# P1 and P2 of the second product in two levels from the third group on, with their factors made inside the kernel

## The chip, the cores and the metric

The kernel runs on one core of a Trainium2 chip. The metric is the device time of one execution in microseconds (us). Engines are named as in the profile: PE multiplies matrices, PEld is its weight load, DVE (VectorE) does elementwise work, ACT (ScalarE) activations and copies, POOL (GpSimd) and SP (SyncE) issue DMAs here.

## The reference

Linear attention with decay over blocks of the sequence, and then a feed-forward layer with a tanh shrink (float32, B=4, H=8, S=768, D=64; 3072 tokens, model width 512, hidden width 2048):

```python
# attention, block by block, with a running state kv
intra = ((qb @ kb.T) * Dmask) @ vb
out_b = intra + (qb * lam_pow) @ kv
kv    = lam_block * kv + (kb * rev_pow).T @ vb
# x: (batch * sequence, heads * D)
h   = x @ w_in          # 3072x512 @ 512x2048: the first product
g   = h - tanh(h)
out = g @ w_out         # 3072x2048 @ 2048x512: the second product
```

## The kernel before

The tokens are taken in six groups, g = 0 to 5, of 512 tokens (128 positions of the sequence in each of the four batches). For each group the attention makes the columns of x, and then come the first and the second product. While group g is multiplied, the attention of group g+1 is worked in between its steps. Group 0 has a path of its own.

**Seven products for eight.** Each product is split in 2 x 2 blocks and done by Strassen's scheme in Winograd's form: seven products P1 to P7 of block sums instead of eight block products. The sums are S1 to S4 on one side and T1 to T4 on the other. The weights' sums for the second product are made during group 0 and lie in DRAM (`factors`).

**Two levels.** For some of the seven products the scheme is applied once more. `TWICE = (3, 5, 6, 4, 7)` names those of the second product; their finer weight factors, seven each in the order `SUB`, lie in DRAM (`fine`). P1 and P2 of the second product are done in one level.

**First product**, `up(g, u, n)`: for each of four units u (512 hidden columns) the products n. A step is four matmuls of 256 columns into one of the PSUM banks: ya or yb for the y sums by the parity of u, z for P5 and P3. DVE and ACT then finish the hidden values `hidden(g, c)` for c in 11, 12, 21, 22: L471 and L467 (for 11), L476, L477 and two L467 (for 22 and 21 after P7), L494, L467, L497 and L498 (for 12 and the sum S1 after P3). L494 reads bank z, and only then may the next unit's P5 write it. From g=2 on, P2 and P4 of the first product are done in two levels (`inner_steps`, L542) ahead of the units.

**Second product.** `down(g, n)` is the form in one level: four pieces of weights, four matmuls of 256 columns for each (L633). `down_twice(g, n, zw)` is the form in two levels: seven steps (x = 1, 2, 6, 5, 7, 3, 4 in this order), each with one piece and four matmuls of 128 columns (L686). `sums_twice` makes the token-side sums s1, s2 and a third one in place ahead of it (L670 to L672), the fourth, s4, is made in between (L691, step x = 3 waits for it), ACT copies each partial sum of y out (L689), and DVE adds the other bank to it (L696, L697).

**Pieces.** Each piece of weights is a 256 KB DMA from DRAM, issued on POOL into a ring of `RING = 7` buffers (tag `wb`), in the fixed order `stream`. A piece can be issued when the buffer that it takes is free; POOL takes its instructions in order.

**Attention of the next group.** `p0` and `p1` are its two halves: `att_transpose` (L331: DVE transposes the 32x32 blocks that SP loads as `q_blk` and `k_blk`, L342 scales), `att_scores` (L352 on PE, L356 on DVE), `att_out` (L400, L406 and copies on ACT), `att_state` (L361, L374, L379, L380). In a group g of 1 to 4, the transposes of p0 stand after unit 2 and its scores after unit 3; the rest follows P2 and later products.

**Order.** In the program P1 of the second product stands in unit 3, between P7 and P3 of the first product (it needs only `hidden(g, 11)`), then P2, P4, P5, P6, P7, P3. The program's order is an input to a scheduler, which fixes the order of instructions on each engine when the kernel is built; each engine then runs its instructions strictly in that order, and waits for the others by semaphores.

```python
INNER = (2, 4)
GI = 2
for g in range(1, NG):
    for u in range(NU):
        for n in ...:                     # up(g, u, n); at n == 1 the next unit's P1
            ...                           # u == 3: every(down(g, 1))
        if not last and u > 1:
            run(p0[u - 2:u - 1])
    every(down(g, 2))
    run(p0[2:])
    every(down_twice(g, 4, "z")); every(down_twice(g, 5, "w")); ...
```

Of the kernel before, what the change touches and what calls it, by code (L numbers as in the profile page):

```python
# [24 lines left out]
def kernel(  # L25
# [157 lines left out]

    SUB = (1, 2, 6, 5, 7, 3, 4)
    GI = 2
    TWICE = (3, 5, 6, 4, 7)
    fine = dram.tile([len(TWICE), len(SUB), 128, NU, 128], F32, name="fine")

    fine_in = dram.tile([2, 3, 128, NU, 128], F32, name="fine_in")
# [62 lines left out]
    def sums_out(kt):  # L252
        x, y = pair[kt]
        b11, b12, b21, b22, t1, t2, t4, t3 = (t[:, i] for t, n in ((x, 2), (y, 6)) for i in range(n))
        for dst, a, b in ((t1, b12, b11), (t2, b22, t1), (t3, b22, b12), (t4, b21, t2)):
            tied(kt > 1, nc.vector.tensor_tensor(dst, a, b, op=AL.subtract))
        f = factors[:].rearrange("x p k c -> p x k c")
        tied(kt > 1, nc.gpsimd.dma_start(out=f[:, 0:1, kt, :], in_=x[:, 0:1, :]))
        tied(kt > 1, nc.gpsimd.dma_start(out=f[:, 1:NX, kt, :], in_=y[:, 0:2, :]))

        for n, j in ((1, 0),) if kt % 2 == 0 else ((2, 0), (3, 1)):
            tied(kt > 1, nc.gpsimd.dma_start(out=fine[:, SUB.index(n), :, kt // 2, :].rearrange("n p c -> p n c"),
                                             in_=y[:, 1:6, ts(j, 128)]))

    def sums_fine(u):
# [234 lines left out]


    INNER = (2, 4)
    toks = {}

    def a_quarter(n, u, i, k):
# [2 lines left out]
    def inner_weights(u):  # L508
        for n in INNER:
            a11, a12, a21, a22 = (a_quarter(n, u, i, k) for i in range(2) for k in range(2))  # L510
            t = late["pool"].tile([128, 4, 128], F32, name="ws2", tag="sums", bufs=4)
            s1, s2, s4 = (t[:, x] for x in range(3))
            for dst, x, y, op in ((s1, a21, a22, AL.add), (s2, s1, a11, AL.subtract), (a21, a11, a21, AL.subtract),
                                  (s4, a12, s2, AL.subtract)):
                tc.keep_in_program_order(nc.vector.tensor_tensor(dst, x, y, op=op))
            nc.gpsimd.dma_start(out=fine_in[INNER.index(n)].rearrange("x p u c -> p u x c")[:, u], in_=t[:, 0:3])

    def inner_tokens(g):
        for n in INNER:
            x = xt[g][FACT[n][1]]  # L520
            b11, b12, b21, b22 = (x[:, k, ts(j, 128)] for k in range(2) for j in range(2))
            t = late["pool"].tile([128, 4, 128], F32, name="tt2", tag="sums", bufs=4)
            t1, t2, t4 = (t[:, x] for x in range(3))
            for dst, x, y in ((t1, b12, b11), (t2, b22, t1), (b12, b22, b12), (t4, b21, t2)):
                nc.vector.tensor_tensor(dst, x, y, op=AL.subtract)
            toks[g, n] = {1: b11, 2: b21, 3: b22, 4: t4, 5: t1, 6: t2, 7: b12}
# [32 lines left out]
    RING = 7  # L559

    def twice(g, n):
        return n in TWICE and not (g == NG - 1 and n == 3)

    def in_turn(g):

# [5 lines left out]
    def pieces_of(g):  # L571
        if g >= GI:
            yield from ((g, ("in", 4), x) for x in (6, 5, 3))
        for n in (1, 2, 4, 5, 6, 7):
            yield from ((g, n, x) for x in (SUB if twice(g, n) else range(NU)))
        if g == NG - 1:
            yield from ((g, 3, x) for x in range(NU))
            return
        for kind, x in in_turn(g):
            if kind == "down":  # L580
                yield g, 3, x
            elif x in (3, 5, 6):
                yield g + 1, ("in", 2), x

    stream = [x for g in range(1, NG) for x in pieces_of(g)]
    sent = {"n": 0}

    def piece(g, n, x):

        i = stream.index((g, n, x))  # L590
        while sent["n"] < min(i + RING, len(stream)):
            g_, n_, x_ = stream[sent["n"]]
            t = late["pool"].tile([128, 2, 256], F32, name="wb", tag="wb", bufs=RING)
            if isinstance(n_, tuple):
# [71 lines left out]

    def sums_twice(g, n):
        a11, a12, a21, a22 = quarter(g, n)
        s1, s2 = (late["pool"].tile([128, NU, 128], F32, name=f"s{x}", tag="sums", bufs=4) for x in (1, 2))
        nc.vector.tensor_tensor(s1, a21, a22, op=AL.add)  # L670
        nc.vector.tensor_tensor(s2, s1, a11, op=AL.subtract)
        nc.vector.tensor_tensor(a21, a11, a21, op=AL.subtract)  # L672
        low[g, n] = (s1, s2)

    def down_twice(g, n, zw):
        a11, a12, a21, a22 = quarter(g, n)
        s1, s2 = low.pop((g, n))
        y = bank("y2", "ya" if n in (4, 6, 3) else "yb", 1)[:, 0:128]
        zw = bank("zw", zw, 1)
        o = res[g, n] = otile(f"q{n}")  # L680
        for x, a, dst, keep in ((1, a11, y, o[:, 0:128]), (2, a12, zw[:, 0:128], None), (6, s2, y, o[:, 128:256]),
                                (5, s1, zw[:, 256:384], None), (7, a21, y, o[:, 384:512]), (3, a12, zw[:, 128:256], None),
                                (4, a22, y, o[:, 256:384])):
            wb = piece(g, n, x).rearrange("p m c -> p (m c)")
            for u in range(NU):
                nc.tensor.matmul(out=dst, lhsT=a[:, u, :], rhs=wb[:, ts(u, 128)], start=x in (1, 2) and u == 0,  # L686
                                 stop=u == NU - 1, skip_group_check=True)
            if keep is not None:
                nc.scalar.activation(keep, dst, AF.Copy)  # L689
            if x == 2:  # L690
                nc.vector.tensor_tensor(a12, a12, s2, op=AL.subtract)  # L691
            if x != STEPS[-1]:
                yield

        o5 = o.rearrange("q (i c) -> q i c", i=2)[:, :, 128:256]
        nc.vector.tensor_tensor(o5, o5, zw[:, 256:384][:, None, :].to_broadcast([128, 2, 128]), op=AL.add)  # L696
        nc.vector.tensor_tensor(o[:, 0:256], o[:, 0:256], zw[:, 0:256], op=AL.add)  # L697
        if n == 6:

            nc.vector.tensor_tensor(o, o, res[g, 1], op=AL.add)  # L700
            for x in (4, 5):
                nc.vector.tensor_tensor(res[g, x], res[g, x], o, op=AL.add)
        elif n == 7:
# [13 lines left out]
    def down_end(g):  # L717
# [4 lines left out]
        for tag, m, c0, c1 in (("z", 0, 0, 256), ("w", 1, 0, 128), ("ya", 1, 128, 256)):  # L722
# [157 lines left out]
    for g in range(1, NG):  # L880
        last = g == NG - 1
        p0, p1 = attention(g + 1) if not last else ([], [])
        for u in range(NU):
            for n in (2, 6, 5, 7, 1, 4, 3) if g < GI else (1, 7, 3) if u == 0 else (6, 5, 1, 7, 3) if u + 1 < NU else (
# [3 lines left out]
                elif u + 1 < NU:  # L888
                    up(g, u + 1, 1)
                else:  # L890
                    every(down(g, 1))
                if g == 1 and u < 2 and n == 5:
                    sums_in(u + 2)
            if g == GI - 1:
                inner_weights(u)
            if not last and u > 1:
                run(p0[u - 2:u - 1])
        if twice(g, 4):
            sums_twice(g, 4)
        every(down(g, 2))  # L900
        run(p0[2:])
        sums_twice(g, 5)
        every(down_twice(g, 4, "z") if twice(g, 4) else down(g, 4))
        run(p1[0:1])
        sums_once(g, 21, 21, 11)
        sums_twice(g, 6)
        every(down_twice(g, 5, "w"))
        run(p1[1:2])
        if twice(g, 7):
            sums_twice(g, 7)  # L910
        every(down_twice(g, 6, "z"))
        if twice(g, 3):
            sums_twice(g, 3)
        run(p1[2:])
        every(down_twice(g, 7, "w") if twice(g, 7) else down(g, 7))
        if last:
            down_end(g)
            continue
        inner_tokens(g + 1)
        p3 = down_twice(g, 3, "z") if twice(g, 3) else down(g, 3)  # L920
# [42 lines left out]
```

## Time and profile before

| | |
|---|---|
| Time, median of 3 runs | 667.03 us (665.2 to 667.34) |
| Profiled execution | 667.09 us, span 665.3 us |
| PE, DVE, ACT, POOL busy | 653.6, 480.0, 215.0, 196.0 us |
| Granted TensorE clock | 1.0 throughout |
| DMA moved | 121.74 MB, mean 183 GB/s |

The span runs from the first to the last instruction of the profiled execution; the time of an execution is 1.8 us longer. A row of the groups gives the line, the engine, the operation, what is written from what, the count, the busy time and the mean of one; two matmul records stand for one float32 matmul. In timelines the first column is the start, the second the length, and brackets give the idle time before and what ended it. Matmul records overlap, so the time of a step is read from start to start.

### The profile page before, as it was taken

The page shows a single profiled execution, that of the slowest core. Times are in us where ns is not written, and L with a number is a line of the kernel's source. Part 1 is how long each engine was busy: PE and PEld are TensorE (multiplying, and loading weights), DVE is VectorE, ACT ScalarE, POOL GpSimd, SP SyncE. Part 2 cuts the span into 40 slices and gives each one's busy share as a digit, 9 for nine tenths or more (in the row PEclk, how much of TensorE's full clock was granted, in tenths as well). Part 3 has the DMA queues.
Part 4 walks back from the last instruction along what each step waited for, and adds up shares of the span by engine and source line. Part 5 has one row for each costly group of instructions (what it writes and reads, how often), then busy time and mean ns, then how long its engine had stood idle before and what let it go on. Part 6 is the DMA issues. An engine that isn't in the chain of part 4 may idle for free.

```text
span 665.3 us, 13244 instructions
## 1 busy us (share of the span) xinstructions
PE 653.6 (98%) x4992; PEld 594.6 (89%) x4992; DVE 480.0 (72%) x869; ACT 215.0 (32%) x413; POOL 196.0 (29%) x340
## 2 busy tenths in 40 slices
PE   7899999999999999999999999999999999999998
PEld 6688888888888899888999988999988899988897
DVE  4467888997787994579895379887368877357753
ACT  4787933423321112341112342112243112233110
POOL 0001425783112445001435101254300245400261
PEclk9999999999999999999999999999999999999999
DMA  9999946997346979435899643698830676610495
GB/s 209 221 209 255 282 159 198 349 332 221 81 87 150 268 214 292 81 71 115 219 265 273 149 76 72 164 297 247 218 68 16 160 237 216 222 38 1 114 303 169
DMA packets 161006, 121.74 MB, mean 183 GB/s; under 512 B 133872, under 2 KB 135024, under 8 KB 160944
## 3 DMA queue, kind: packets, MB, share of 16 engines
q0 software_dynamic: 26400, 86.27, 41.0%
q1 hardware_dynamic: 134400, 34.64, 26.0%
q8 instruction: 39, 0.64, 0.4%
q14 instruction: 23, 0.19, 0.1%
q10 hardware_dynamic: 144, 0.00, 0.0%
HBM read 100.67 MB, written 20.19 MB: 182 GB/s over the span
## 4 chain that ended last, share of the span: by engine, by line
PE 74%; issue 9%; DVE 6%; DMA 4%; POOL 3%; SPq 2%; ACT 2%; POOLq 0%; DVEq 0%; ACTq 0%
PE y L458 13%; PE y L686 12%; PE zw L686 9%; PE z L458 8%; PE h L741 7%; PE y L542 4%; PE w L633 4%; PE y L633 4%; PE sp L352 3%; PE op L406 2%; PE z L542 2%; PE op L400 1%; PE w L542 1%; PE end L725 1%; DMA fine<-wt 1%
## 5 line engine op out<-in xcount | busy, mean ns | idle before, releaser
L598 POOL DMA_DIRECT2D wb<-fine x168 | 90.5, 538 | 137.3 <-PE y L686 60.8
L466 ACT ACTIVATE th<-g 128x512 f32<-128x512 f32 x76 | 47.6, 630 | 99.5 <-DVE g L471 34.2
L689 ACT ACTIVATE q<-y 128x128 f32<-128x128 f32 x96 | 26.6, 278 | 149.3 <-PE y L686 148.5
L458 PE MATMUL y<-xt,w 128*128 128x256 f32 x320 | 73.5, 380 | 0.0
L601 POOL DMA_DIRECT2D wb<-factors x44 | 23.8, 542 | 165.0 <-PE y L633 127.8
L458 PEld LDWEIGHTS y<-xt,w 128*128 128x128 f32 x320 | 59.9, 190 | 8.5 <-ACT g L546 0.9
L467 DVE TENSOR_TENSOR g<-g,th 128x512 f32<-128x512 f32 x76 | 52.1, 689 | 21.1 <-ACT th L466 21.0
L686 PE MATMUL y<-wb,g 128*128 128x128 f32 x456 | 60.6, 278 | 0.0
L741 PE MATMUL h<-xt,w 128*128 128x256 f32 x256 | 58.0, 383 | 2.5 <-DVE w L296 2.5
L741 PEld LDWEIGHTS h<-xt,w 128*128 128x128 f32 x256 | 47.7, 190 | 10.3 <-DVE w L296 2.9
L686 PEld LDWEIGHTS y<-wb,g 128*128 128x128 f32 x456 | 55.1, 192 | 1.3 <-issue 0.3
L686 PE MATMUL zw<-wb,g 128*128 128x128 f32 x304 | 40.3, 275 | 0.1
L458 PE MATMUL z<-tt,ws 128*128 128x256 f32 x160 | 38.1, 381 | 0.0
L458 PE MATMUL y<-tt,ws 128*128 128x256 f32 x160 | 37.8, 379 | 0.0
L458 PE MATMUL z<-xt,ws 128*128 128x256 f32 x160 | 37.8, 379 | 0.0
L686 PEld LDWEIGHTS zw<-wb,g 128*128 128x128 f32 x304 | 37.0, 192 | 0.2 <-DVE g L691 0.2
L633 PE MATMUL w<-wb,g 128*128 128x256 f32 x160 | 35.8, 382 | 0.0
L633 PE MATMUL y<-wb,g 128*128 128x256 f32 x160 | 35.3, 379 | 0.0
L356 DVE TENSOR_TENSOR ss<-sp,mask 128x512 f32<-128x512 f32 x48 | 31.1, 685 | 5.8 <-PE sp L352 5.8
L458 PEld LDWEIGHTS z<-xt,ws 128*128 128x128 f32 x160 | 30.4, 190 | 4.1
L633 PEld LDWEIGHTS y<-wb,g 128*128 128x128 f32 x160 | 30.4, 190 | 4.1
L633 PEld LDWEIGHTS w<-wb,g 128*128 128x128 f32 x160 | 30.1, 190 | 4.4
(178 smaller groups left out, 1292.8 us busy)
## 6 DMA issues: line engine op xcount, KB each, us to landing
wb<-fine POOLq DMA_DIRECT2D x168, 256.0 KB, 4.0
wb<-factors POOLq DMA_DIRECT2D x44, 256.0 KB, 4.3
v_nat<-in_v_dram SPq DMA_DIRECT2D x24, 256.0 KB, 5.2
wb<-fine_in POOLq DMA_DIRECT2D x24, 256.0 KB, 4.2
k_nat<-in_k_dram SPq DMA_DIRECT2D x20, 256.0 KB, 5.0
raw<-in_moe_w_out_dram POOLq DMA_DIRECT2D x10, 512.0 KB, 5.4
raw<-in_moe_w_in_dram SPq DMA_DIRECT2D x8, 512.0 KB, 6.1
raw<-in_moe_w_in_dram SPq DMA_DIRECT2D x16, 256.0 KB, 6.1
```

Of the source, the lines that this page charges most:

```text
L352: tied(g == 0, nc.tensor.matmul(out=sp[j][:, p, :], lhsT=kt[ts(j, 64), p, :], rhs=qt[ts(j, 64), p, :], start=True, stop=True))
L356: tied(g == 0, nc.vector.tensor_tensor(ss[:, j], sp[j], mask[:, j], op=AL.mult))
L458: nc.tensor.matmul(out=t[:, m, :], lhsT=wt[:, kt, ts(m, 128)], rhs=x[:, kt, :], start=first and m == 0 and kt == 0, stop=kt == 1, skip_gro ...
L466: nc.scalar.activation(th, src, AF.Tanh)
L467: nc.vector.tensor_tensor(dst(c), src, th, op=AL.subtract)
L542: nc.tensor.matmul(out=dst[:, ts(u, 128)], lhsT=a, rhs=b, start=x in (1, 2, 5) and u == 0, stop=True, skip_group_check=True)
L598: nc.gpsimd.dma_start(out=t.rearrange("p m c -> p (m c)"), in_=fine[TWICE.index(n_), SUB.index(x_)].rearrange("p u c -> p (u c)"))
L601: nc.gpsimd.dma_start(out=t, in_=factors[XAT[FACT[n_][1]]][:, 2 * x_:2 * x_ + 2, :])
L633: nc.tensor.matmul(out=t[:, m, :], lhsT=a[:, u, kt, ts(m, 128)], rhs=wb[:, kt, :], start=first and u == 0 and m == 0 and kt == 0, stop=u = ...
L686: nc.tensor.matmul(out=dst, lhsT=a[:, u, :], rhs=wb[:, ts(u, 128)], start=x in (1, 2) and u == 0, stop=u == NU - 1, skip_group_check=True)
L689: nc.scalar.activation(keep, dst, AF.Copy)
L741: tied(u == 0, nc.tensor.matmul(out=hm[c][:, m, :], lhsT=w1[u][:, i, a, ts(m, 128)], rhs=xt[0, t][:, i, :], start=m == 0 and i == 0, stop= ...
```

## The change

`TWICE` also holds 1 and 2, from g=2 on. Their factors for the second level are made in g=2 itself: the four quarters of `factors` for P1 are loaded through the ring as pieces of their own, three of them are written to `fine` as they are, four DVE subtractions make the others, and these are written too. That happens in units 1 (for P1) and 2 (for P2) of the first product, one subtraction at each of four steps. P1 and P2 then read seven pieces each. Their sums s3 and s4 get buffers of their own instead of being made in place, since their operands are needed again. The next group's first transposes stand after unit 0 and its first scores after unit 1. The banks z and w change places for the later products.

```diff
-    TWICE = (3, 5, 6, 4, 7)
+    TWICE = (3, 5, 6, 4, 7, 1, 2)
...
     def twice(g, n):
-        return n in TWICE and not (g == NG - 1 and n == 3)
+        return g >= GI if n in (1, 2) else g < NG - 1 or n != 3
...
+        if g == GI:
+            yield from ((g, ("quarter", n), x) for n in (1, 2) for x in range(4))
...
+    def factors_twice(g, n):
+
+        at, quarters = fine[TWICE.index(n)], []
+        for x, direct in enumerate((1, None, 2, 3)):
+            quarters.append(piece(g, ("quarter", n), x).rearrange("p m (v c) -> p (m v) c", v=2))
+            if direct:
+                nc.gpsimd.dma_start(out=at[SUB.index(direct)], in_=quarters[x])
+        b11, b12, b21, b22 = quarters
+        t1, t2, t4 = (late["pool"].tile([128, NU, 128], F32, name=f"wt{x}", tag="sums", bufs=SUMS) for x in (1, 2, 4))
+        for x, dst, a, b in ((5, t1, b12, b11), (6, t2, b22, t1), (7, b12, b22, b12), (4, t4, b21, t2)):
+            tc.keep_in_program_order(nc.vector.tensor_tensor(dst, a, b, op=AL.subtract))
+            nc.gpsimd.dma_start(out=at[SUB.index(x)], in_=dst)
+            yield
...
     def sums_twice(g, n):
         a11, a12, a21, a22 = quarter(g, n)
-        s1, s2 = (late["pool"].tile([128, NU, 128], F32, name=f"s{x}", tag="sums", bufs=4) for x in (1, 2))
+        s1, s2, s3 = (late["pool"].tile([128, NU, 128], F32, name=f"s{x}", tag="sums", bufs=SUMS) if x < 3 or n < 3 else a21
+                      for x in (1, 2, 3))
...
     def down_twice(g, n, zw):
...
+        s4 = late["pool"].tile([128, NU, 128], F32, name="s4", tag="sums", bufs=SUMS) if n < 3 else a12
-        y = bank("y2", "ya" if n in (4, 6, 3) else "yb", 1)[:, 0:128]
+        y = bank("y2", "ya" if n in (1, 4, 6, 3) else "yb", 1)[:, 0:128]
...
-        if n == 6:
+        if n == 2:
+            nc.vector.tensor_tensor(o, o, res[g, 1], op=AL.add)
+            store(g, 11, o)
+            sums_once(g, 11, "S1", 11)
+        elif n == 6:
...
-                    every(down(g, 1))
+                    every(down_twice(g, 1, "w") if twice(g, 1) else down(g, 1))
...
+                if g == GI and u in (1, 2) and n in (6, 5, 1, 7):
+                    if n == 6:
+                        making = factors_twice(g, u)
+                    next(making)
+                if u + 1 == NU and n == 5 and twice(g, 1):
+                    sums_twice(g, 1)
...
-            if not last and u > 1:
-                run(p0[u - 2:u - 1])
-        if twice(g, 4):
-            sums_twice(g, 4)
-        every(down(g, 2))
+            early_ = u if g >= GI else u - 2
+            if not last and 0 <= early_ < 2:
+                run(p0[early_:early_ + 1])
+        even = ("w", "z") if twice(g, 2) else ("z", "w")
+        if twice(g, 2):
+            sums_twice(g, 2)
+        sums_twice(g, 4)
+        every(down_twice(g, 2, "z") if twice(g, 2) else down(g, 2))
...
-        every(down_twice(g, 4, "z") if twice(g, 4) else down(g, 4))
+        every(down_twice(g, 4, even[0]))
```

More of the change, by code (lines that the diff above doesn't have):

```diff
@@ L261, in sums_out @@
         for n, j in ((1, 0),) if kt % 2 == 0 else ((2, 0), (3, 1)):
-            tied(kt > 1, nc.gpsimd.dma_start(out=fine[:, SUB.index(n), :, kt // 2, :].rearrange("n p c -> p n c"),
+            tied(kt > 1, nc.gpsimd.dma_start(out=fine[0:5, SUB.index(n), :, kt // 2, :].rearrange("n p c -> p n c"),
                                              in_=y[:, 1:6, ts(j, 128)]))
@@ L502 @@
     INNER = (2, 4)
+    SUMS = 4
     toks = {}
@@ L510, in inner_weights @@
             a11, a12, a21, a22 = (a_quarter(n, u, i, k) for i in range(2) for k in range(2))
-            t = late["pool"].tile([128, 4, 128], F32, name="ws2", tag="sums", bufs=4)
+            t = late["pool"].tile([128, 4, 128], F32, name="ws2", tag="sums", bufs=SUMS)
             s1, s2, s4 = (t[:, x] for x in range(3))
@@ L521, in inner_tokens @@
             b11, b12, b21, b22 = (x[:, k, ts(j, 128)] for k in range(2) for j in range(2))
-            t = late["pool"].tile([128, 4, 128], F32, name="tt2", tag="sums", bufs=4)
+            t = late["pool"].tile([128, 4, 128], F32, name="tt2", tag="sums", bufs=SUMS)
             t1, t2, t4 = (t[:, x] for x in range(3))
@@ L593, in piece @@
             t = late["pool"].tile([128, 2, 256], F32, name="wb", tag="wb", bufs=RING)
-            if isinstance(n_, tuple):
+            if isinstance(n_, tuple) and n_[0] == "quarter":
+                i, j = divmod(x_, 2)
+                nc.gpsimd.dma_start(out=t.rearrange("p m (v c) -> p (m v) c", v=2), in_=factors[
+                    XAT[FACT[n_[1]][1]]].rearrange("p (u m) c -> p u m c", m=2)[:, :, i, ts(j, 128)])
+            elif isinstance(n_, tuple):
                 nc.gpsimd.dma_start(out=t.rearrange("p m c -> p (m c)"), in_=fine_in[
@@ L668, in sums_twice @@
         a11, a12, a21, a22 = quarter(g, n)
-        s1, s2 = (late["pool"].tile([128, NU, 128], F32, name=f"s{x}", tag="sums", bufs=4) for x in (1, 2))
+        s1, s2, s3 = (late["pool"].tile([128, NU, 128], F32, name=f"s{x}", tag="sums", bufs=SUMS) if x < 3 or n < 3 else a21
+                      for x in (1, 2, 3))
         nc.vector.tensor_tensor(s1, a21, a22, op=AL.add)
         nc.vector.tensor_tensor(s2, s1, a11, op=AL.subtract)
-        nc.vector.tensor_tensor(a21, a11, a21, op=AL.subtract)
-        low[g, n] = (s1, s2)
+        nc.vector.tensor_tensor(s3, a11, a21, op=AL.subtract)
+        low[g, n] = (s1, s2, s3)
     def down_twice(g, n, zw):
         a11, a12, a21, a22 = quarter(g, n)
-        s1, s2 = low.pop((g, n))
-        y = bank("y2", "ya" if n in (4, 6, 3) else "yb", 1)[:, 0:128]
+        s1, s2, s3 = low.pop((g, n))
+        s4 = late["pool"].tile([128, NU, 128], F32, name="s4", tag="sums", bufs=SUMS) if n < 3 else a12
+        y = bank("y2", "ya" if n in (1, 4, 6, 3) else "yb", 1)[:, 0:128]
         zw = bank("zw", zw, 1)
-        o = res[g, n] = otile(f"q{n}")
+        o = res[g, n] = late["pool"].tile([128, 512], F32, name="o11", tag="o11", bufs=1) if n == 2 else otile(f"q{n}")
         for x, a, dst, keep in ((1, a11, y, o[:, 0:128]), (2, a12, zw[:, 0:128], None), (6, s2, y, o[:, 128:256]),
-                                (5, s1, zw[:, 256:384], None), (7, a21, y, o[:, 384:512]), (3, a12, zw[:, 128:256], None),
+                                (5, s1, zw[:, 256:384], None), (7, s3, y, o[:, 384:512]), (3, s4, zw[:, 128:256], None),
                                 (4, a22, y, o[:, 256:384])):
@@ L690, in down_twice @@
             if x == 2:
-                nc.vector.tensor_tensor(a12, a12, s2, op=AL.subtract)
+                nc.vector.tensor_tensor(s4, a12, s2, op=AL.subtract)
             if x != STEPS[-1]:
@@ L721, in down_end @@
         wbs = [piece(g, 3, u) for u in range(NU)]
-        for tag, m, c0, c1 in (("z", 0, 0, 256), ("w", 1, 0, 128), ("ya", 1, 128, 256)):
+        for tag, m, c0, c1 in (("w", 0, 0, 256), ("z", 1, 0, 128), ("ya", 1, 128, 256)):
             t = bank("end", tag, 1)[:, 0:c1 - c0]
@@ L906 @@
         sums_twice(g, 6)
-        every(down_twice(g, 5, "w"))
+        every(down_twice(g, 5, even[1]))
         run(p1[1:2])
-        if twice(g, 7):
-            sums_twice(g, 7)
-        every(down_twice(g, 6, "z"))
+        sums_twice(g, 7)
+        every(down_twice(g, 6, even[0]))
         if twice(g, 3):
@@ L914 @@
         run(p1[2:])
-        every(down_twice(g, 7, "w") if twice(g, 7) else down(g, 7))
+        every(down_twice(g, 7, even[1]))
         if last:
@@ L919 @@
         inner_tokens(g + 1)
-        p3 = down_twice(g, 3, "z") if twice(g, 3) else down(g, 3)
+        p3 = down_twice(g, 3, even[0])
         p2 = inner_steps(g + 1, 2, "yb")
```

## The prediction

> **What bounds the kernel now.** I read the page's busy times and costliest groups, then PE's timeline through one group, then DVE's busy time by stage, DVE's timeline, and the DMA issues.
>
> ```profile
> PE 653.6 (98%) x4992; PEld 594.6 (89%) x4992; DVE 480.0 (72%) x869; ACT 215.0 (32%) x413; POOL 196.0 (29%) x340
> ```
>
> PE is busy for 653.6 of 665.3 us, so the time is PE's work plus its pauses. PE's timeline (start, us, engine, line, operands, count; two records per matmul) in the third group, g=2:
>
> ```profile
> 299.64 1.89 PE L458 MATMUL y<-xt,w 128*128 128x256 f32 x8
> 301.37 7.07 PE L633 MATMUL y<-wb,g 128*128 128x256 f32 x32
> 308.27 1.89 PE L458 MATMUL z<-xt,ws 128*128 128x256 f32 x8
> 310.09 2.06 PE L352 MATMUL sp<-qt,kt 64*128 64x128 f32 x32
> 312.08 7.17 PE L633 MATMUL w<-wb,g 128*128 128x256 f32 x32
> 319.18 1.10 PE L400 MATMUL op<-qd,state 64*64 64x128 f32 x32
> ...
> 323.04 1.16 PE L686 MATMUL y<-wb,g 128*128 128x128 f32 x8
> 324.04 1.06 PE L686 MATMUL zw<-wb,g 128*128 128x128 f32 x8
> 324.93 1.06 PE L686 MATMUL y<-wb,s 128*128 128x128 f32 x8
> ```
>
> P1 runs 301.37 to 308.27: 16 matmuls of 256 columns, 0.432 us each. A step of the two-level form is four matmuls of 128 columns in 0.893 us (324.04 to 324.93). PE has no gap of note. DVE by stage (stage, its length, busy, clock, DMA share, GB/s):
>
> ```profile
> 274.00:301.00 27.00, 19.92 (x31) 1.00 0.32 59
> 301.00:323.00 22.00, 20.64 (x35) 1.00 0.58 132
> ```
>
> Where P1 and P2 run, DVE is busy 20.64 of 22 us: it has 1.4 us to give. Its timeline there gives the prices:
>
> ```profile
> 304.11 0.68 DVE L476 TENSOR_TENSOR g<-g,y 128x512 f32<-128x512 f32 x1
> 304.70 0.68 DVE L477 TENSOR_TENSOR g<-g,y 128x512 f32<-128x512 f32 x1
> ...
> 310.20 0.69 DVE L494 TENSOR_TENSOR g<-g,z 128x512 f32<-128x512 f32 x1 [0.60 <-PE z L458]
> 311.64 0.69 DVE L467 TENSOR_TENSOR g<-g,th 128x512 f32<-128x512 f32 x1 [0.76 <-ACT th L466]
> ```
>
> One operation starts every 0.60 us; 0.72 if it reads the one before (L497 to L498, 290.56 to 291.28); add, tanh, subtract takes 1.44 from start to start (310.20 to 311.64).
>
> **What is removed: PE.** P1 or P2 costs 16 x 0.432 = 6.90 us now and 7 x 0.893 = 6.25 in two levels. That is 0.65 per product, 1.30 per group, 5.2 over groups 2 to 5. The weight loads of the new form (28 x 0.192 = 5.4 us by the L686 rows) stay under it.
>
> In the Trainium skill, "TensorE: Matmul & The Clock Gate", section "Back-to-back issue gap", speaks against this: in a stream of load and matmul pairs it gives about 81 ns per matmul at 128 columns and 131 at 512. Interpolated (an estimate from that page), 128 columns would cost 0.83 of 256, and a two-level product 28 x 0.83 x 0.432 = 10.0 us, 25 us lost in all.
>
> The trace decides otherwise: 0.223 us against 0.432, a ratio of 0.52, in rows of this same code (L686).
>
> **What is added: DVE.** Per group eight operations of 128x512 (s1, s2, s3, s4 of P1 and of P2) at 0.60, and four PSUM additions of 256 columns at about 0.4 (L696, L697): 6.4 us. Moved out to units 0 and 1 are six transposes and scalings (300.53 to 304.11, 3.6 us) and four mask products (2.4 us). The stage would hold 20.64 + 6.4 - 6.0 = 21.0 us of DVE work in 22 - 1.3 = 20.7. DVE is as long as PE there, so every place where PE needs a DVE result must be walked, in the order of the changed program.
>
> *Fourth group, g=3.* Clock 0 is 382.06, where unit 0's P3 of the first product starts; each first-product step takes 1.73, scores 1.99. DVE reaches L498 of unit 0 at 5.56 (387.62). The transposes then take it to 9.74, and 14 operations at 0.60 follow: it starts unit 3's L471 at 18.13, L467 at 19.57 and, six operations later, unit 2's L494 at 23.17, ending 23.86. PE wants bank z for unit 3's P5 at 23.45: **0.46 lost**. P1 then finds its sums (s4 ends at 26.3, wanted at 31.2). After P7 of unit 3 (27.37) DVE does L476, L477, two L467, s1, s2, s3 of P2, L696, s1 of P4, L697 and three L620, and only at 35.25 the L494 that frees bank z, although PE ended that step at 34.67. P2's first step and four L400, which the new order puts behind it, keep PE busy to 36.03, and z is free at 35.99. Then L467 36.69, L497 37.41, L498 38.13, two sums of P4, s4 of P2 39.93 to 40.62. PE wants s4 at 40.5: 0.17. L400 now breaks P2 twice, and each passage to or from 64-row matmuls shows 0.10 (334.88 to 335.87 is 0.99 instead of 0.893): 0.4. **P2 loses 0.57.** P4 starts at 45.4. Its L696 comes 6.1 us after that, against 5.73 in the trace (323.04 to 328.77); behind it stand six transposes and then the L691 that P5's step 3 needs. PE is there 10.72 after P4's start, the trace's L691 ends at 10.80, the new one at 11.1: **0.33 more**. Sum 1.36 against 1.30: -0.06.
>
> *g=4:* no decay and no state (L361, L379) for the group after, so P5 isn't late: 0.46 + 0.57 lost, +0.27. *g=5:* no scores or transposes: z for unit 3's P5 0.19 late, P2's step 6 waits 0.43 for ACT's copy and z, s4 0.03: 0.65 lost, +0.65.
>
> *g=2* makes the factors: eight more DVE operations among units 1 to 3. Unit 1's L494 slips to 14.54, ends 15.23, and P5 of unit 2 wants z at 14.14: 1.14. P1 finds bank ya late by 0.29 and P5 of unit 3 z by 0.11. P2's s4 costs 0.43, P5's step 3 0.35. Sum 2.32: -1.02.
>
> All: -1.02 - 0.06 + 0.27 + 0.65 = -0.16, so 0.2 us slower.
>
> **Queues.** POOL gets 22 more DMAs in g=2 (eight quarter loads, fourteen writes) and 6 more pieces per group. The trace shows no such write in that stage, where the DMA share is 0.32:
>
> ```profile
> wb<-factors POOLq DMA_DIRECT2D x44, 256.0 KB, 4.3
> fine<-f POOLq DMA_DIRECT2D x16, 256.0 KB, 5.5
> out_dram<-o POOLq DMA_DIRECT2D x6, 256.0 KB, 3.6
> ```
>
> The tight one: P1's seventh piece takes the ring slot of P2's B12, which is written out first (issued at 24.8 on g=2's clock). PE needs the piece at 33.6, so write and load have 8.7 us. With 3.6 + 4.1 they take 7.7, with 5.5 + 4.3 9.8 (1.1 late), with the longest landings that the trace has for fine and wb (9.4 and 7.3) 16.7 (8 late). It can't gain. I take 0, nearest to the stores in a quiet stage. All of P2's pieces stand on POOL behind that wait. In other groups P1's seven pieces lie in the ring long before, and P2's are issued while P1 runs; the trace's whole loss to late pieces is 2.0 us in 28 products, so at most 0.07 for each of the 8, 0.5.
>
> SP: the blocks that the sooner transposes read were issued by 259.5 and 361.0 and are wanted near 283 and 388, over 20 us of cover. The last k block waits for a slot that the transposes free (issued at 301.26 after the transpose at 300.53) and moves up with them, and the k and v loads behind it too; only 0.2 us of PE ever waited for those. Zero. ACT gets four copies of 0.28 for one of 0.60; each hides behind a step of 0.893. Zero, but for the 0.43 counted.
>
> **The numbers.** The profiled execution took 667.09 (span 665.3 and 1.8 around it); the median of the runs is 667.03. 667.09 + 0.16 is 667.2. About 0.3% (2 us) is what a measurement of this kernel can tell from no change.
>
> *Rival 1, the cover holds.* DVE's idle 1.4 us and the 7 us free in units 0 and 1 take the work, and PE waits only where the factors are made: 667.1 - 5.2 + 1.0 = 662.9; half of it, 665. For: PE waits almost nowhere on DVE now. Against: DVE's ledger above, in a fixed order. 0.20.
>
> *Rival 2, slower: the seventh piece.* If writing and reading back take more than 8.7 us, PE stands in P1 with P2's pieces queued behind. At 5.7 + 5.8 it is 2.8 late and the time 670.0; at the longest landings 675. For: fine<-f took 5.5. Against: the quiet stage. 0.18.
>
> *Rival 3, no cheaper on PE:* excluded by the L686 rows.
>
> The forecast, gain given back to DVE, has 0.62: 0.44 within 0.3%, 0.06 below it (a wait or two of 0.5 not there), 0.12 above (one more wait of 0.6 per group). Faster 0.20 + 0.06 = 0.26, same 0.44, slower 0.18 + 0.12 = 0.30. The range runs from 663.8, inside rival 1, to 670.6, past rival 2's 670.0.
>
> **What would show it.** Right: P1 and P2 steps at 0.893; DVE busy over 95% from P1 to P4; PE waiting on L494's and s4's lines, 0.4 to 0.6 per place; g=2's P5 of unit 2 late by about 1.1; g=5 shorter by 0.65. Wrong: no PE waits on DVE there (rival 1); PE waiting for a piece in P1 of g=2 (rival 2); steps longer than 0.893.

## The result, and the profile after

The changed kernel takes 674.17 us (median of 6 runs, 673.02 to 675.79), the kernel before 667.18 beside it on the same chip: a ratio of 1.0107, 95% interval 1.0083 to 1.0131. Run once more on another chip it was 1.0082 (1.0052 to 1.0111). The change costs 5.5 to 7 us. The prediction said 667.2 and at most 670.6, so it was wrong. The profiled execution took 674.02 us with a span of 672.2, against 667.09 and 665.3 before.

The busy times of the changed kernel answer to the line shown of before:

```profile
PE 655.6 (98%) x5184; PEld 598.0 (89%) x5184; DVE 506.4 (75%) x925; ACT 221.9 (33%) x441; POOL 223.1 (33%) x386
```

PE's busy time has not fallen, and the span has grown by 6.9: PE waits. A stage view (DVE's busy time; stage, length, busy, clock, DMA share, GB/s) shows P1 and P2 of g=2, where DVE was busy 20.64 of 22.00 us:

```profile
303.17:326.00 22.83, 22.31 (x39) 1.00 0.83 257
```

DVE is now full (98%), and the DMA share has gone from 0.58 to 0.83. PE's timeline of the same group:

```profile
293.52 1.99 PE L458 MATMUL z<-tt,ws 128*128 128x256 f32 x8 [0.80 <-DVE g L494]
...
315.74 0.45 PE L400 MATMUL op<-qd,state 64*64 64x128 f32 x8
316.12 1.16 PE L709 MATMUL zw<-wb,g 128*128 128x128 f32 x8
317.11 1.06 PE L709 MATMUL y<-wb,s 128*128 128x128 f32 x8
318.01 1.06 PE L709 MATMUL zw<-wb,s 128*128 128x128 f32 x8
318.90 1.06 PE L709 MATMUL y<-wb,s 128*128 128x128 f32 x8
319.89 0.45 PE L400 MATMUL op<-qd,state 64*64 64x128 f32 x8
```

P2's undisturbed steps follow each other by 0.89, as predicted. L400 cuts P2. The step behind a cut or a wait reads 1.16 instead of 1.06, and its successor comes 0.99 later: **each interruption of PE costs 0.10 beyond its own length**. The wait for z in unit 2 is there (0.80 idle; PE starts 0.96 late, which the prediction put at 1.14), and DVE does at that place what the prediction walked through, making (L601) and first product in turn:

```profile
290.98 0.69 DVE L601 TENSOR_TENSOR wb<-wb 128x512 f32<-128x512 f32 x1
291.58 0.68 DVE L477 TENSOR_TENSOR g<-g,y 128x512 f32<-128x512 f32 x1
292.18 0.69 DVE L467 TENSOR_TENSOR g<-g,th 128x512 f32<-128x512 f32 x1
292.78 0.68 DVE L494 TENSOR_TENSOR g<-g,z 128x512 f32<-128x512 f32 x1
```

What the prediction did not have is at the end. PE's timeline, then POOL's:

```profile
661.08 1.10 PE L752 MATMUL end<-wb,g 128*128 128x256 f32 x4 [0.82 <-DMA wb<-factors]
662.58 6.43 PE L752 MATMUL end<-wb,g 128*128 128x256 f32 x44 [0.40 <-DMA wb<-factors]
```

```profile
653.19 0.54 POOL L619 DMA_DIRECT2D wb<-fine  x1 [0.35 <-PE zw L709]
654.09 0.54 POOL L619 DMA_DIRECT2D wb<-fine  x1 [0.35 <-PE y L709]
657.44 2.13 POOL L622 DMA_DIRECT2D wb<-factors  x4 [2.82 <-PE y L709]
```

POOL issues a piece every 0.89 us until 654.6, then nothing for 2.82 us, then four in a row. The view names PE as the releaser, but the step that frees this slot ended at 654.70, and the other semaphore that this DMA waits for last moved at 653.68: **POOL stopped for 2.75 us with everything it waits for already there.** The first of the four landed at 660.94. PE wanted it at 660.10 and started 0.98 later.

To separate this from what differs from one execution to the next, I read each trace by groups: from the start of the last L543 matmul (L542 before) ahead of a group to that ahead of the next; the last column runs to the span's end. All columns are us from PE's timeline.

| kernel | ahead of g=2 | g=2 | g=3 | g=4 | g=5 and end |
|---|---|---|---|---|---|
| before | 273.5 | 104.93 | 104.93 | 103.11 | 78.86 |
| changed | 274.6 | 107.95 | 105.53 | 103.27 | 80.90 |
| changed, once more | 273.8 | 107.53 | 105.53 | 103.28 | 81.28 |
| predicted change | 0 | +1.02 | +0.06 | -0.27 | -0.65 |
| measured change | +1.1, +0.4 | +3.0, +2.6 | +0.60 | +0.16 | +2.0, +2.4 |

The first column moves by itself: ten executions of the changed kernel and of variants whose PE work is the same up to there lie between 271.6 and 274.6. The two traces of the changed kernel agree to 0.02 us in g=3 and g=4, so these columns can tell tenths apart. In g=2 and in the last column the two differ by 0.4, and a smaller difference there, from one trace of each kernel, decides nothing.

"By the starts" below means: how much later than an undisturbed step (0.89, or 1.73 in the first product) the next one starts. That is more than the idle time in brackets, since matmul records overlap.

### The profile page after: what moved, and what is told of

It reads as the page before. It is cut to its first block, busy times and chain, and to the rows that moved or that the text cites. A ratio compares the mean times of both kernels' runs of the same rounds, so it can differ in the third digit from the quotient of the medians.

```text
span 672.2 us, 13848 instructions
## 1 busy us (share of the span) xinstructions
PE 655.6 (98%) x5184; PEld 598.0 (89%) x5184; DVE 506.4 (75%) x925; ACT 221.9 (33%) x441; POOL 223.1 (33%) x386
## 4 chain that ended last, share of the span: by engine, by line
PE 40%; issue 20%; DVE 13%; DMA 10%; POOL 8%; SPq 6%; ACT 2%; POOLq 0%; DVEq 0%; ACTq 0%
PE y L709 10%; PE zw L709 8%; POOL wb L619 5%; PE h L768 5%; SPq L143 3%; PE y L543 3%; PE y L458 3%; DMA raw<-in_moe_w_in_dram 2%; PE op L406 2%; DVE g L467 2%; DMA fine<-wt 2%; DMA wb<-fine 2%; PE sp L352 2%; DMA wb<-factors 2%; PE z L543 2%
## 5 line engine op out<-in xcount | busy, mean ns | idle before, releaser
L619 POOL DMA_DIRECT2D wb<-fine x224 | 120.9, 540 | 254.6 <-PE y L709 179.0
L712 ACT ACTIVATE q<-y 128x128 f32<-128x128 f32 x112 | 31.1, 278 | 163.5 <-PE y L709 162.4
L709 PE MATMUL y<-wb,g 128*128 128x128 f32 x584 | 79.1, 278 | 0.1
L709 PEld LDWEIGHTS y<-wb,g 128*128 128x128 f32 x584 | 72.0, 192 | 2.8 <-ACT o L712 0.7
L709 PE MATMUL zw<-wb,g 128*128 128x128 f32 x368 | 49.2, 276 | 0.4 <-DVE g L494 0.4
L709 PE MATMUL y<-wb,s 128*128 128x128 f32 x320 | 42.9, 277 | 0.7 <-ACT o L712 0.4
L709 PE MATMUL zw<-wb,s 128*128 128x128 f32 x320 | 42.9, 276 | 0.1
L709 PEld LDWEIGHTS y<-wb,s 128*128 128x128 f32 x320 | 39.0, 192 | 1.3 <-ACT o L712 0.6
L709 PEld LDWEIGHTS zw<-wb,s 128*128 128x128 f32 x320 | 39.0, 192 | 0.7 <-DVE s L714 0.6
L458 PEld LDWEIGHTS z<-tt,ws 128*128 128x128 f32 x160 | 29.3, 190 | 6.5 <-DVE g L494 3.0
L458 PEld LDWEIGHTS y<-tt,ws 128*128 128x128 f32 x160 | 29.8, 190 | 4.1
```

The lines of the kernel that those rows point to most:

```text
L458: nc.tensor.matmul(out=t[:, m, :], lhsT=wt[:, kt, ts(m, 128)], rhs=x[:, kt, :], start=first and m == 0 and kt == 0, stop=kt == 1, skip_gro ...
```

## The experiments

Theories: **1** (formed on the two traces): POOL's stops, the making and L400's cuts carry the loss. **2** (formed after the first runs): late pieces belong to the change. Against both, the prediction's ledger, in which DVE alone takes the gain back.

**The stop at the end: stores of group 0 on SP.**

```
-        eng = nc.sync if g == NG - 1 else nc.gpsimd
+        eng = nc.sync if g in (0, NG - 1) else nc.gpsimd
```

> The changed kernel, with the four output stores of group 0 issued by SP instead of POOL. In the changed kernel's trace POOL, with every release it waits for already there, stops for 2.2 to 2.75 us at three places (322.18, 476.89, 657.44), each about 100 DMAs of 128 rows after the one before; the last stop falls on the four pieces of the end, and PE stands for them (0.82 and 0.40 idle, about 1.8 us in all). Theory 1 (the stop comes by the amount of DMA work that POOL has issued): with 8 DMAs' worth less issued by POOL, the stop falls behind its last DMA, the end costs PE nothing, and the time is 674.2 - 1.8 = 672.4. Rival (the end's pieces are late because of the order in which P7's steps give ring slots back): the stop stays where it is, 674.2.

Measured: 681.74 us, 1.0194 (1.0172 to 1.0217), a miss as a time: PE stood 8.04 us in group 1 for DVE (L714). That the loads behind the stores on SP made DVE late there was not tested. The columns still answer: the stop has left the end (POOL's last one ends at 530.65), and g=5 and end take 79.62 instead of 80.90 to 81.28.

**Without the making.**

```
-                if g == GI and u in (1, 2) and n in (6, 5, 1, 7):
-                    if n == 6:
-                        making = factors_twice(g, u)
-                    next(making)
...
-                                    in_=fine[TWICE.index(n_), SUB.index(x_)].rearrange("p u c -> p (u c)"))
+                                    in_=fine[TWICE.index(n_) % 5, SUB.index(x_)].rearrange("p u c -> p (u c)"))
```

> The changed kernel without the making: no quarter loads, no subtractions, no writes of P1's and P2's factors; P1 and P2 read the stored factors of two other products in their place. Theory 1 (making costs what g=2 lost beyond g=3 in the traces, 3.0 against 0.4, and by the amount of POOL's DMA work it also puts POOL's stop on the end's pieces, 1.8): 674.2 - 2.6 - 1.8 = 669.8. Theory 2, the prediction's ledger (g=2 loses 0.96 more than g=3, POOL nothing): 673.2. Rival (the two-level form itself loses in every group): 674 less at most 1.

Measured: 669.88 us, 1.0022 (1.0006 to 1.0039), near theory 1. g=2 takes 105.88, g=5 and end 79.88. POOL's stop has moved away from the end, as theory 1 said, and lies where pieces are not urgent (POOL's timeline in g=2's last product; four loads follow in a row):

```profile
367.33 2.12 POOL L617 DMA_DIRECT2D wb<-fine  x4 [2.70 <-PE zw L707]
```

**L400's cuts, first try: outputs ahead of P2.**

```
-        every(down_twice(g, 2, "z") if twice(g, 2) else down(g, 2))
-        run(p0[2:])
+        if twice(g, 2):
+            run(p0[2:])
+            every(down_twice(g, 2, "z"))
+        else:
+            every(down(g, 2))
+            run(p0[2:])
```

> The changed kernel with the second half of the next group's transposes, scores and outputs put ahead of P2 instead of behind it, from g=2 on; on PE the four-matmul pieces of L400 no longer cut P2 in three. Theory 1 (each cut costs about 0.4 us: 0.09 into L400, 0.13 inside it, 0.19 out of it, against the 0.2 of the prediction; two cuts in each of g=2, 3, 4): 674.2 - 2.4 = 671.8. Prediction's price of 0.2 per cut: 673.0. Rival (DVE sets the time there, and the cuts only fill PE's waits): no change, 674.2, or slower because P2 then waits for DVE without them.

Measured: 676.46 us, 1.0120 (1.0099 to 1.0140): not the 671.8 of theory 1. The cuts are gone, but L374 now stands inside P2 and waits for DVE (0.90 <-DVE k_nat L361 in g=3, 0.59 in g=2), and more pieces come late: g=2 takes 109.34, g=3 107.58.

**Without P1's and P2's sums.**

```
+        if n < 3:
+            low[g, n] = (a21, a22, a11)
+            return
...
-        s4 = late["pool"].tile([128, NU, 128], F32, name="s4", tag="sums", bufs=SUMS) if n < 3 else a12
+        s4 = a12
...
-            if x == 2:
+            if x == 2 and n > 2:
```

> The changed kernel without the eight DVE operations per group that make s1 to s4 of P1 and P2 (the quarters of the hidden values themselves stand in their place); PE, ACT and POOL do what they did. The prediction's ledger (the gain is given back to DVE): it takes away 0.43 + 0.35 in g=2, up to 1.36 in g=3, 1.03 in g=4 and 0.65 in g=5, so 674.2 - 3.8 = 670.4. Theory 1 (most of the loss lies at POOL's stops, the making and the cuts of P2): the listed waits of the changed trace that the sums can take away are 0.44 + 0.39 in g=3, 0.44 in g=4, 0.53 in g=5 and 0.2 in g=2, together 2.0: 672.2. Rival (DVE is not waited for): 674.2.

Measured: 668.20 us, 0.9998 (0.9979 to 1.0016), below all three. g=4 falls from 103.27 to 102.23, g=3 from 105.53 to 104.74. So the eight DVE operations cost PE about 1.0 in g=4, not the 0.44 that the changed trace lists as waits. They bring L400's cuts with them: the scheduler, which orders PE's instructions when the kernel is built, puts L400 in one run behind P2 here. In g=3 the gain is smaller because pieces come late there without the sums: by the starts three steps lose 0.24, 0.21 and 0.37 (from 436.60 to 439.86, where the view names the DMA).

**Neither making nor sums.** Both edits together.

> The changed kernel without the making and without the eight DVE operations per group for s1 to s4 of P1 and P2 (factors of other products and the quarters themselves stand in their place). What is left of the change is PE's: 28 matmuls of 128 columns for 16 of 256 in each product, and the cuts that L400 makes in P2. Theory 1 (PE keeps its 5.2, less six cuts at 0.4, and POOL's stop falls away from the end's pieces as in the run without the making): 2.8 below the kernel before, a ratio of 0.996. The prediction's rival 1 without its price for the making: 5.2 below, 0.992. Rival (the two-level form brings nothing on PE): 1.000.

Measured: 663.84 us, 0.9953 (0.9931 to 0.9975), theory 1's number. The columns give PE's side: g=2 104.03, g=3 104.04, g=4 102.22, each 0.89 to 0.90 below before. That is not 1.30 less L400's cuts, since L400 cuts nothing here either, and the agreement with theory 1 is luck. PE's timeline of g=2, P1 and then P2:

```profile
303.39 1.05 PE L710 MATMUL y<-wb,g 128*128 128x128 f32 x8
304.29 1.06 PE L710 MATMUL zw<-wb,g 128*128 128x128 f32 x8
305.23 1.16 PE L710 MATMUL y<-wb,g 128*128 128x128 f32 x8
306.23 1.06 PE L710 MATMUL zw<-wb,g 128*128 128x128 f32 x8
...
311.53 1.05 PE L710 MATMUL y<-wb,g 128*128 128x128 f32 x8
312.47 1.16 PE L710 MATMUL zw<-wb,g 128*128 128x128 f32 x8
...
318.03 1.10 PE L400 MATMUL op<-qd,state 64*64 64x128 f32 x32
```

P1 and P2 lose 0.15 each at their first steps (0.94 and 1.00 for 0.89), and one step of the first product, the P5 of unit 3, loses 0.10, as it does in the run below with the transposes alone moved: 1.30 - 0.40 = 0.90. What causes the 0.15 was not tested. g=5 and end gain only 0.39.

**L400's cuts, second try: P2 in one run.**

```
-                nc.tensor.matmul(out=dst, lhsT=a[:, u, :], rhs=wb[:, ts(u, 128)], start=x in (1, 2) and u == 0,
+                tied(n == 2, nc.tensor.matmul(out=dst, lhsT=a[:, u, :], rhs=wb[:, ts(u, 128)], start=x in (1, 2) and u == 0,
...
-                            nc.tensor.matmul(out=dst(n, pp, j), lhsT=state[r, b, pp, :], rhs=tr[g, b][2][r, pp, :],
+                            tied(g > GI and half == 0, nc.tensor.matmul(
```

> The changed kernel with the order on PE of P2's matmuls and of the first sixteen L400 written out, so that L400 stands in one run behind P2's last step; P4's first steps move up beside P2, everything else is left. Theory 1 (a cut costs 0.4: 0.09 into L400, 0.13 inside, 0.19 out of it, and 0.10 at the next matmul; six cuts in all, of which the first of each group also fills a wait for z of 0.25): 1.0107 less 2.4 - 0.75 = 1.6 us, a ratio of 1.008. Prediction's price of 0.2 per cut: 1.010. Rival (L400 only fills waits for DVE): 1.011.

Measured: 672.63 us, 1.0069 (1.0048 to 1.0091), which cannot be told from the changed kernel. The columns can: g=3 takes 105.52 and g=4 103.26, as with the cuts. P2's second step in g=3, changed kernel and this one:

```profile
422.58 1.16 PE L709 MATMUL zw<-wb,g 128*128 128x128 f32 x8 [0.18 <-DVE g L494]
```

```profile
421.72 1.16 PE L710 MATMUL zw<-wb,g 128*128 128x128 f32 x8 [0.56 <-DVE g L495]
```

What the cuts had cost, PE now waits for DVE. By the starts in g=4, P2 loses 1.07 with the cuts (0.35 and 0.41 for two of them, each the way into L400, the way out and the tail of 0.10; 0.25 for z; 0.06 at a later step) and 1.06 without (0.82 and 0.24, at two steps). Theory 1's 0.4 per cut is the right price and gains nothing: DVE sets the time there; the cuts filled its waits (the rival).

**Eight ring slots.**

```
-    RING = 7
+    RING = 8
+    made = set()
...
+        cap = min([stream.index((GI, m, 1)) for m in (1, 2) if m not in made] or [len(stream)])
-        while sent["n"] < min(i + RING, len(stream)):
+        while sent["n"] < min(i + RING, cap):
```

> The changed kernel with eight ring slots for pieces instead of seven (and no piece of P1 or P2 issued in g=2 before it is made). Theory 1 (PE waits at the end and in g=2's P4 to P6 because a stop of POOL of 2.2 to 2.75 us and a landing of about 4 us together pass the 6.25 us that seven steps give): one more step of 0.89 takes 0.9 of the end's 1.8 and the 0.77 of g=2, 1.6 us in all, a ratio of 1.008. Rival (late pieces are a matter of the DMA share, not of the look-ahead): 1.011.

Measured: 670.76 us, 1.0050 (1.0032 to 1.0068), more than theory 1 expected: g=2 takes 106.58 (1.0 to 1.4 less), g=3 and g=4 do not move (105.52, 103.26), g=5 and end 80.27, with POOL's stop still before the end's pieces.

**The sooner transposes alone, on the kernel before.**

```
-            if not last and u > 1:
-                run(p0[u - 2:u - 1])
+            early_ = u if g >= GI else u - 2
+            if not last and 0 <= early_ < 2:
+                run(p0[early_:early_ + 1])
```

> The kernel before with one part of the change alone: the next group's first transposes, scalings and scores two units sooner from g=2 on. The prediction has it at nothing on PE (SP's loads have over 20 us of cover, a passage to the scores costs the same 0.2 + 0.2 wherever it stands): ratio 1.000. Theory 1 says the same. Rival (the moved DVE work of 6 us makes the first product's L494 late in units 0 and 1 in each of three groups, 0.3 to 0.5 each): 1.002 to 1.004.

Measured: 668.62 us, 1.0011 (0.9993 to 1.0029): no difference that can be told from none, nor from the rival's lower figure. The columns tell more: g=2 to g=4 take 105.27, 105.85 and 103.22, and g=5 and end 79.44, so 0.34, 0.92, 0.11 and 0.58 longer than before, 1.95 in all. About 0.1 in each of g=2 to g=4 is the unit-3 step named above, and 0.8 in g=3 by the starts is the late piece, which took 5.6 us to land. The rest is in small pauses for which the trace names no piece. The move is not free.

**The changed kernel with the transposes back** (`early_ = u - 2`).

> The changed kernel with the transposes and scores where the kernel before has them (units 2 and 3). The prediction's ledger: 6.0 us of DVE work come back into a stage where it has 21.0 for 20.7 us, so PE waits up to 6 more in each of g=2, 3, 4; half of that, 3 per group, is the least I expect: a ratio of 1.024. Rival (where they stand matters little, as the run with the transposes alone moved cost 0.7): 1.010.

Measured: 679.24 us, 1.0157 (1.0113 to 1.0202). g=2 takes 113.31, g=3 107.36, g=4 104.38. Moving them was worth 5.4, 1.8 and 1.1: the ledger's direction, but less than 3 per group in g=3 and g=4, which both theories missed.

**Eight slots in the kernel before** (`RING = 8`, nothing else).

> The kernel before with eight ring slots for pieces instead of seven, and nothing else. Theory 2 (late pieces belong to the change: with all seven products in two levels PE takes 256 KB every 0.89 us from P1 to P7, where the one-level P1 and P2 took it every 1.73 and let the ring run ahead): the kernel before gains no more than the 1.5 us for which its group 1 waits, a ratio of 0.998 to 1.000. Rival (eight slots help both kernels alike, as they did the changed one by 3.8): 0.994.

Measured: 666.23 us, 0.9969 (0.9950 to 0.9989). Only the stretch ahead of g=2 shortens, which moves by itself by more than that; g=2 to g=4 are 104.93, 104.93, 103.11 and the end 78.84, so an eighth slot is worth nothing to the kernel before in the groups that the change touches: theory 2. This version is faster than both kernels, by about 2 us than the kernel before.

**Eight slots without the making.**

> The changed kernel without the making (P1 and P2 read factors of two other products) and with eight ring slots. Theory 2 (late pieces cost in every group, without the making too: its run with seven slots lists 0.31, 0.36, 0.34 from g=3 on and about 0.5 in group 1, each with 0.1 behind it): 1.0022 less 1.5 to 2.0 us, a ratio of 0.9995. Rival (the eighth slot only covers the making in g=2 and POOL's stop before the end): 1.002.

Measured: 668.59 us, 1.0011 (0.9989 to 1.0032); theory 2's and the rival's figures both lie in it. The groups say that without the making the slot is worth 0.36 in g=2 and nothing in g=3 and g=4 (105.83, 103.26), so theory 2 was wrong there. The late piece in g=2 is gone, but then PE waits in P5 for DVE (L712; 0.55 by the starts in g=2, 0.86 in g=3): the late pieces had filled a wait that was coming anyway.

**P1 alone in two levels, eight slots.**

```
-        return g >= GI if n in (1, 2) else g < NG - 1 or n != 3
+        return g >= GI if n == 1 else False if n == 2 else g < NG - 1 or n != 3
...
-                if g == GI and u in (1, 2) and n in (6, 5, 1, 7):
+                if g == GI and u == 1 and n in (6, 5, 1, 7):
```

> The changed kernel with P1 alone in two levels from g=2 on, made in unit 1 of g=2 with half the loads and writes, P2 in one level, and eight ring slots. By the prices measured so far: PE gains 0.65 in each of four groups and L400 cuts nothing (2.6), the four sums and two PSUM additions fit into what the moved transposes leave of DVE, half the making costs about 1.2: 1.4 below the kernel before, a ratio of 0.998. Rival (DVE's order, not its amount, makes PE wait for z in unit 3, so half the waits stay, 0.7 per group): 1.002.

Measured: 666.79 us, 0.9987 (0.9963 to 1.0010), not told apart from before, nor from the kernel before with eight slots. g=3 and g=4 gain 0.26 each, not 0.65: the wait for z in unit 3 takes 0.39 by the starts (L494), so even half of the sums takes more than half of the gain.

**The making's two halves.** The first keeps loads and subtractions, the second loads and writes:

```
-            if direct:
-                nc.gpsimd.dma_start(out=at[SUB.index(direct)], in_=quarters[x])
...
-            nc.gpsimd.dma_start(out=at[SUB.index(x)], in_=dst)
```

> The changed kernel with the making's quarter loads and DVE subtractions, but without its fourteen writes (P1 and P2 read factors of two other products, so nothing waits for the made ones). Theory 2 (two prices: the subtractions cost PE its waits for z in units 1 and 2, 0.96 + 0.24 and 0.1 behind each, 1.4 us; the writes cost what is left, late pieces in g=2 and POOL's stop before the end): g=2 takes 107.3, and the kernel 1.0022 + 1.4 us, a ratio of 1.004 to 1.005. Rival (the subtractions are all of it): g=2 107.95, ratio 1.008 or more.

```
-            tc.keep_in_program_order(nc.vector.tensor_tensor(dst, a, b, op=AL.subtract))
-            nc.gpsimd.dma_start(out=at[SUB.index(x)], in_=dst)
+            nc.gpsimd.dma_start(out=at[SUB.index(x)], in_=b12 if x == 7 else a)
```

> The changed kernel with the making's loads and writes as they are, but without its eight DVE subtractions (the quarters are written in their place), so POOL's queue, the DMA amount and the order of writes and pieces stay. Theory 2: the waits for z in units 1 and 2 are gone (1.4), the late pieces of g=2 and the end stay: g=2 takes 106.5, the ratio is 1.0107 less 1.4 us, 1.0086. Rival (the subtractions are all of it): g=2 105.9, ratio 1.002 to 1.004.

Measured: 670.41 us, 1.0057 (1.0037 to 1.0078), g=2 106.81; and 670.92 us, 1.0061 (1.0037 to 1.0084), g=2 105.67. Theory 2 misses with both (107.3 and 106.5 for g=2, 1.0086 for the second ratio); the rival's 105.9 for the second g=2 is nearer. Against 105.88 without the making, the subtractions cost 0.9, the writes by themselves nothing that can be told from none, and both together 1.7 to 2.1.

These differences are not prices of single waits, for PE's late pieces change with them. POOL's timeline of g=2 in the changed kernel invites an explanation by the writes:

```profile
309.44 3.98 POOL L619 DMA_DIRECT2D wb<-fine  x7 [2.60 <-DMA fine<-wb]
```

POOL stands behind the write of B12, then issues seven pieces in 3.98 us. P1 itself did not stand for its seventh piece, but PE waits for a piece later in the group, at the first step of P5. That wait stands in the kernel without the making too (changed kernel, then without the making):

```profile
332.91 1.16 PE L709 MATMUL y<-wb,gS 128*128 128x128 f32 x8 [0.47 <-DMA wb<-fine]
```

```profile
331.26 1.16 PE L707 MATMUL y<-wb,gS 128*128 128x128 f32 x8 [0.53 <-DMA wb<-fine]
```

So it comes neither from the burst nor from the making. What goes with it is how long this piece takes to land. POOL issues it when the first step of P4 has freed its slot, 4.9 us before PE wants it (327.39 to 332.28 in the changed kernel). It landed in 5.4 to 5.6 us in the changed kernel (both times), without the making, and with loads and writes alone: all four wait. It landed in 4.7 with loads and subtractions and without making and sums, in 4.0 before: none of these waits. Why it lands later in some kernels is open. The writes are not needed for it, and in g=3 moving the transposes alone brought such a landing (5.6) and such a wait.

By the starts, what the making adds in g=2 beyond the kernel without it is 1.06 at z of unit 2, 0.3 to 0.7 in P1, and 0.4 where a first piece of L352 cuts P5, less 0.1 in P2: the subtractions and the order on PE that comes with them. With the subtractions alone the late piece of P5 shrinks to about 0.25, and so they seem to cost only 0.9.

**The changed kernel once more.**

> The changed kernel as it is, once more. Every theory: 1.0107, and g=2, 3, 4 within 0.1 us of 107.95, 105.53 and 103.27; what differs lies before the first product of group 1.

Measured: 673.02 us, 1.0082 (1.0052 to 1.0111); its groups stand in the table. g=2 came 0.42 below, outside the 0.1 that was expected.

**Where POOL stops.** I added up the rows that POOL's DMA records name (128 for a 256 KB piece, 512 for a quarter load, 256 for a store) to each such stop:

| kernel | rows issued by POOL before each stop | stops at, us |
|---|---|---|
| before | 41,600; 55,168 | 375.19; 572.59 |
| changed | 41,856; 55,552; 69,120 | 322.18; 476.89; 657.44 |
| without the making | 41,472; 54,912 | 367.33; 556.41 |
| the making's loads and writes | 41,856; 55,552; 69,120 | 318.55; 472.76; 653.64 |

It stops 2.2 to 2.75 us every 13,400 to 13,700 rows in all of them, wherever that falls in time. The third stop comes at about 69,000 rows. The changed kernel issues 69,632 from POOL and the kernel before 60,672, so the making and the finer pieces brought that stop into the program, onto the pieces of the end. The eight traces with a stop there (the changed kernel twice, both tries on the cuts, no sums, the making's loads and writes, the transposes back, eight slots) take 80.27 to 81.99 for g=5 and the end, 81.2 in the mean; the five that make sums but have no stop there (stores on SP, both without the making, P1 alone, the making's subtractions) take 79.38 to 79.92, 79.7 in the mean. So the stop costs about 1.4. Of the eight, one makes no sums (80.50); its fellow without a stop, neither making nor sums, takes 78.47. What POOL does in it stays open. The Trainium skill, "DMA: Bandwidth & Descriptors", section "Terms", says that descriptors that software generates (SWDGE) are written to rings in SBUF. A turn of such a ring would fit a count by rows, but no run here shows it.

## Why the prediction was wrong

The first three bullets name the steps that failed, the largest first.

- **Late pieces, "at most 0.5", failed.** The prediction spread the 2.0 us that the trace before loses to late pieces over 28 products. All of that lies ahead of g=2; from there to the end the kernel before waits for no piece. In the changed kernel the end's pieces cost 1.7 by the starts, the first piece of P5 in g=2 0.9, and part of g=5's small pauses comes on top. At the end the cause is POOL's third stop: the finer pieces and the making put 8,960 more rows on POOL. That a number of rows moves a stop of POOL was not in the prediction at all, though its trace had two such stops (POOL idle 2.68 ahead of 375.19). In g=2 the cause is a landing of 5.5 us against 4.0 before, and why is open.
- **P2's 0.57 was half of what it costs.** By the starts P2 loses 1.07 in g=4 and as much in g=3. Two cuts cost 0.35 and 0.41 where the prediction had 0.20 each; its walk had bank z free 0.04 before PE wants it, and PE lost 0.25 there; s4, put at 0.17, cost at most 0.06. The other terms held: z of unit 3 0.29 + 0.10 (0.46 predicted), P5's L714 in g=3 0.39 (0.33). With these, g=4 is -1.30 + 0.39 + 1.07 = +0.16, as measured, where -0.27 was predicted; g=3 is +0.55 (measured +0.60, predicted +0.06). The prediction had the 0.10 behind a wait in hand (0.99 instead of 0.893) and used it for cuts alone. Its waits each hold about 0.05 more than the numbers shown with them, and it does not say why.
- **g=2: P1 and P5.** z of unit 2 was right (0.96 + 0.10, predicted 1.14). P1 and the first product's P5 of unit 3, put at 0.40 together, lost 0.7 to 1.05 by the starts; steps of the first product now cut P1. P2, put at 0.43, lost about 0.9. At P5 the predicted 0.35 for s4 did not come; the late piece (0.9) and a cut by the first piece of L352 (0.4) did. With -1.30 for the steps that is +2.6 to +3.0, as measured.
- **"The seventh piece, I take 0" came out, and rival 2 did not:** PE did not stand in P1 for it. The prediction could not choose between 7.7 and 16.7 us for write and load, so this was in part luck.
- **PE's gain per step was right, and its sum too large.** Steps run at 0.893, but without making and sums g=2, 3 and 4 gain 0.90, 0.89 and 0.89 and not 1.30, for the three small losses shown with that run. In the changed kernel P1 loses nothing in g=3 and g=4, and the 1.30 holds. The estimate that the prediction weighed from the Trainium skill, "TensorE: Matmul & The Clock Gate", section "Back-to-back issue gap" (25 us lost), did not hold: the decision by L686's rows was right.
- **The direction of the DVE ledger was right.** From the run without making and sums to the changed kernel g=3 is 1.49 longer and g=4 1.05. The ledger, cuts included, had 1.36 and 1.03, but its parts differ as said.
- **g=5.** Predicted 0.65 shorter, measured 2.0 to 2.4 longer. By the starts on PE in the changed trace it is -1.30 from the steps, +0.24 at z of unit 3, +0.63 for ACT's copy ahead of P2's third step (0.43 predicted), about +0.7 in small pauses of P2 to P7, and +1.7 at the end's pieces, behind POOL's stop. The trace names no cause for most of the small pauses; without the making it names late pieces for two of them. Even without making and sums g=5 gains only 0.39.
- **"Transposes: zero"** holds for the ratio (1.0011, not told from 1) and not for the columns, which are 1.95 longer with the move alone, 0.8 of it for one late piece. What the move saves is in the ledger's direction: without it g=2, 3 and 4 are 8.3 longer together, though the ratios (1.0157 against 1.0107, from two chips, with wide intervals) give 3.3.
- **Rival 1** (662.9, with 1.0 for the making) is near what the kernel does with DVE's part free: 663.8 measured without making and sums. Its reason "PE waits almost nowhere on DVE now" was true, and no argument for a stage with 1.4 us to give.

Added up with the two traces: g=2 2.0, g=3 0.5, g=4 0.4, g=5 and end 2.7 above the prediction, and 1.1 ahead of g=2 that is not the change's (0.4 in the second execution). What stays open: what POOL does in its stops, why pieces land in 4.0 to 4.7 us in some kernels and 5.4 to 5.7 in others at the same place, and the 0.15 that P1 and P2 lose at their first steps without the sums.

## What to carry to other kernels

When an edit trades PE work for work of an engine that is already full in that stage, PE's gain is given away there; make the ledger of that stage, and add to each new wait the tail that the profile shows behind old ones (0.10 here). When an edit adds DMAs to a queue, ask not only whether a piece is late where it is added, but how long before its use each piece can be issued at all, and where the queue's periodic stops will then fall. Before a cause is given to a wait, look for the same wait in the run without that cause. Compare traces by groups between fixed points of the program: here g=3 and g=4 repeated to 0.02 us while whole runs scattered by 3.

## What the runs showed of the hardware that was not expected

POOL stops for 2.2 to 2.75 us after every 13,400 to 13,700 rows of DMA that it issues. At the end, where its waits could be followed, they were met. With seven slots a piece can be issued 5.4 us before its use (654.70 to 660.10), which does not cover a stop of 2.74 and a landing of 3.50 together. PE's first two-level step after a wait or a cut takes 0.99 to the next instead of 0.89, for DVE, ACT and DMA alike.
